# One reciprocal of eight columns for both units of a q tile, and the first token chunk's operands begun one queue turn later

## The chip, the cores and the metric

The kernel runs on one core of a Trainium2 chip. Its time is the device time of one execution in microseconds (us). The engines of the core work side by side, each through its own list of instructions in a fixed order: TensorE (PE in the profile, with the weight loads as PEld), VectorE (DVE), ScalarE (ACT), GpSimd (POOL) and SyncE (SP), which here only issues DMA transfers.

## The reference

A linear attention on random features feeds two feed-forward blocks without a residual. Scales of the inputs and shapes are left out where they don't matter.

```python
# attention: batch 4, heads 8, seq 576, head_dim 64, 128 features
phi(x) = exp(h - max(h)) / sqrt(128),  h = x @ omega.T - |x|^2 / 2      # x = q or k, scaled
q_p, k_p = phi(q), phi(k)
kv  = einsum('bhsm,bhsd->bhmd', k_p, v)
z   = sum(k_p, axis=2)
num = einsum('bhsm,bhmd->bhsd', q_p, kv)
den = einsum('bhsm,bhm->bhs', q_p, z)[..., None] + 1e-06
x   = (num / den) as [2304 tokens, 512]
# first block: 512 -> 2048 -> 512
x = softplus(x @ w_in) @ w_out
# second block: 512 -> 1024 (twice), 1024 -> 1024, 1024 -> 512
out = (((x @ w1) * (x @ w2)) @ w3) @ w_out
```

Everything is float32, and the output must be close to the float32 result.

## The kernel before, in words

**Precision and tiling.** A float32 product on TensorE is made of three matmuls of operands that were split into a high part (a rounded cast, name ending in h) and a low part (the value less its high part, name ending in l). Tokens are worked on in 18 q tiles of 128. The attention results of six tiles make one token chunk of 768, of which there are 3. The products of the feed-forward blocks go by Strassen-like quads: of each chunk of x four corner pieces (a11, a12, a21, a22) and four sums (s1 to s4) are made and split into high and low parts. All matmul results go to a pool of 8 PSUM banks (`ps()`, L83), so an early matmul often waits until VectorE or ScalarE has read a bank that is seven tiles old.

**Stages.** From 0 to 57 us the features of k and the sums kv are made, and weights are unpacked. From 57 to 150 us comes the q stage, on which the change acts. After it follow, on TensorE almost alone, the two feed-forward blocks, to 807 us.

**The q stage.** A tile has two units of 4 heads. For each unit, `q_feat` (L393) projects q (six matmuls), VectorE finds the row maximum (nmax, L349), and ScalarE applies four exponentials (qp, L354). `q_turn` (L406) transposes qp on TensorE (L409) and ScalarE copies the result (qpt, L411). `q_num` (L413) multiplies qpt with kv into one PSUM bank of 4 x 65 columns. The 65th column of each head is the denominator. VectorE adds a constant to the four denominators (den, L426), takes the reciprocal (L427, 128x4) and multiplies (xt, L430). `x_turn` (L435) transposes xt (L439), VectorE or ScalarE copies it (xs, L442 or L444), and SP stores it to xd in HBM (L445). The loop over tiles (L767) does step t of the projection, step t-2 of `q_turn`, t-3 of the numerators and t-4 of `x_turn`. In odd steps the numerators come first and in even steps last, so that the numerators of two tiles stand side by side on TensorE: 64 short matmuls into four banks.

**Operands of a chunk.** `operands` (L448) makes a list of small steps for a chunk: two loads of 768 KB from xd (xq, L455, into a pool of 2 buffers that all chunks share), then GAP empty steps (L483, only for chunks 0 and 1), then the casts on ScalarE (high parts, L469), the sums s1 to s4 on VectorE (L462) and the low parts on VectorE (L472). The first xq holds a11 and a21, the second a12 and a22. A queue takes some of these steps after each unit of the q stage (`step`, L241; JOB_Q = 0.5 steps a unit before the first chunk's list is there, 1.2 after). Chunk 0's list is queued after the turn of tile 5, chunk 1's after that of tile 11, chunk 2's behind the loop. In the loop's last steps (FILL, L754) the first quad (Up1 of chunk 0) is begun between the last tiles.

**Order.** The program is handed to a scheduler that sets the order on each engine from its own estimate, so a small change in the source can reorder instructions on several engines. Evictions of the quads (u, c and p: L517, L524, and the softplus L557) have a raised priority.

Of the kernel before, what the change touches and what calls it, by code (L numbers as in the profile page):

```python
# [19 lines left out]
F32 = mybir.dt.float32  # L20
# [4 lines left out]
ALU = mybir.AluOpType  # L25
AX = mybir.AxisListType

B, H, S, D = 4, 8, 576, 64
M = 128
NT = B * S  # L30
# [31 lines left out]
KEEP = 4  # L62
WARM = 3
WO_AHEAD = 3
GAP = 3
FILL = [18, 19, 20]
URGENT = 300
LINE = 32
# [3 lines left out]
def body(ctx: ExitStack, tc: tile.TileContext, q, k, k_rest, v, v_rest, om_t, w_in, w_out, w12, w3, wo, out):  # L72
    nc = tc.nc
    cp = ctx.enter_context(tc.tile_pool(name="cp", bufs=1))
    sm = ctx.enter_context(tc.tile_pool(name="sm", bufs=1))
    M_ = ctx.enter_context(tc.tile_pool(name="M_", bufs=14))
# [6 lines left out]
    def ps():  # L83
        return ps_.tile([128, 512], F32, tag="ps", name="ps")
# [7 lines left out]
    def tt(name):  # L92
        return T_.tile([128, 1024], F32, tag="t", name=name)

    def matmul(o, a, b, start, stop, **kw):
        nc.tensor.matmul(out=o, lhsT=a, rhs=b, start=start, stop=stop, **kw)  # L96
# [7 lines left out]
    xd = dr.tile([128, KD, NT], F32, name="xd")  # L104
# [10 lines left out]
    def take(pool, n):  # L115
        def ok():
            return free[pool] >= n

        return ok


    class Job:
# [5 lines left out]
        def load(self):  # L128
            self.raw = L_.tile([128, 4 * self.n], I16, tag="l", name="raw")
            (self.queue or nc.scalar).dma_start(out=self.raw[:, :4 * self.n - 1], in_=self.src.bitcast(I16)[:, 1:])  # L130
# [143 lines left out]
    def pair(name, bufs):  # L274
        n = small.get(name, (None, 1))[1]
        if n:
            small[name] = sm.tile([128, 2, 4], F32, tag=name, bufs=bufs, name=name), 0
        else:
            small[name] = small[name][0], 1
        return small[name][0][:, 1 - bool(n)]  # L280
# [6 lines left out]
    def xslot(pool, n, dt, name):  # L287
        return pools[pool].tile([128, n], dt, tag="x", name=name)

    kt, vt, kps, kpr, kvs, qts, kacc, raw = {}, {}, {}, {}, {}, {}, {}, {}  # L290
# [84 lines left out]
    def matmul_half(o, a, b, start, stop):  # L375
        for c in range(0, a.shape[-1], HALF):
            matmul(o[c:c + HALF], a[:, c:c + HALF], b, start, stop, skip_group_check=True)
# [11 lines left out]
        nc.scalar.copy(out=kvs[b][:, 4 * g:4 * g + 4, :], in_=acc)  # L389

    qp, qpt, xt = {}, {}, {}

    def q_feat(u):  # L393
        t, g = divmod(u, 2)
        p = project(lambda p: [x[:, 2 * g + p, :] for x in qts[t]])
        if g and t >= NT // 128 - len(EARLY):
            free["X0"] += 2

        def exps():
            qp[u] = M_.tile([128, 4, M], F32, tag="m", name="qp")  # L400
            features(*p, qp[u])

        waiting.append(exps)
        flush(QLAG)
# [5 lines left out]
        qpt[u] = M_.tile([128, 4, 128], F32, tag="m", name="qpt")  # L410
        nc.scalar.copy(out=qpt[u], in_=tp.rearrange("p (h t) -> p h t", h=4))  # L411

    def q_num(u):  # L413
        t, g = divmod(u, 2)
        nm = ps()
        nm = nm[:, 0:4 * (D + 1)].rearrange("p (h d) -> p h d", h=4)
        lo, hi = 128 * t, 128 * t + 128
        for h in range(4):
            a = lo
            while a < hi:  # L420
                b = a // S
                e = min(hi, (b + 1) * S)
                matmul_half(nm[a - lo:e - lo, h, :], qpt[u][:, h, a - lo:e - lo], kvs[b][:, 4 * g + h, :], True, True)
                a = e
        den = pair("den", 3)[:, :, None]
        nc.vector.tensor_scalar(out=den, in0=nm[:, :, D:D + 1], scalar1=1e-6 * M, scalar2=None, op0=ALU.add)  # L426
        nc.vector.reciprocal(out=den, in_=den)  # L427
        if g == 0:
            xt[t] = M_.tile([128, H, D], F32, tag="m", name="xt")
        nc.vector.tensor_tensor(  # L430
            out=xt[t][:, 4 * g:4 * g + 4, :], in0=nm[:, :, 0:D],
            in1=den.to_broadcast([128, 4, D]), op=ALU.mult,
        )

    def x_turn(t):  # L435
        tp = ps()
# [11 lines left out]
    def operands(c, src, pool):  # L448

        o, a, s = {}, [], {}  # L450

        def load(kk):
            def op():
                r = L_.tile([128, 2, 2 * N], F32, tag="l", name="xq")
                nc.sync.dma_start(out=r, in_=src[:, 2 * kk:2 * kk + 2, 2 * N * c:2 * N * (c + 1)])  # L455
                a.append([r[:, :, 0:N], r[:, :, N:2 * N]])
            return (op, lambda: stored[0] >= 2 * N * (c + 1)) if src is yd else op

        def total(name, x, y, op_):
            def op():  # L460
                s[name] = tt(name)[:, 0:2 * N].rearrange("p (k t) -> p k t", k=2)
                nc.vector.tensor_tensor(out=s[name], in0=x(), in1=y(), op=op_)  # L462
            return op

        def parts(name, x):
            def op_hi():
                free[pool] -= 2
                o[name] = [xslot(pool, 2 * N, FR, f"x{name}{w}").rearrange("p (k t) -> p k t", k=2) for w in "hl"]
                nc.scalar.copy(out=o[name][0], in_=x())  # L469

            def op_lo():
                nc.vector.tensor_tensor(out=o[name][1], in0=x(), in1=o[name][0].bitcast(F32), op=ALU.subtract)  # L472

            return [(op_hi, take(pool, 2)), op_lo]

        a11, a21 = lambda: a[0][0], lambda: a[0][1]
        a12, a22 = lambda: a[1][0], lambda: a[1][1]
        hi, lo = {}, {}
        for name, x in (("a11", a11), ("a12", a12), ("a22", a22), *((n, lambda n=n: s[n]) for n in ("s1", "s2", "s3", "s4"))):
            hi[name], lo[name] = parts(name, x)  # L480
        s1, s2 = total("s1", a21, a22, ALU.add), total("s2", lambda: s["s1"], a11, ALU.subtract)
        s3, s4 = total("s3", a11, a21, ALU.subtract), total("s4", a12, lambda: s["s2"], ALU.subtract)
        ops = [load(0), load(1)] + [lambda: None] * (GAP if src is xd and c < 2 else 0)  # L483
        if src is xd:
            ops += [hi["a11"], s3, lo["a11"], hi["s3"], s1, lo["s3"], s2, hi["s1"], hi["s2"], lo["s1"], lo["s2"]]
        else:
            ops += [hi["a11"], s1, lo["a11"], s2, s3, hi["s2"], lo["s2"], hi["s3"], hi["s1"], lo["s3"], lo["s1"]]
        ops += [hi["a12"], s4, lo["a12"], hi["a22"], hi["s4"], lo["a22"], lo["s4"]]
        ops.append(lambda: ready.add(c))
        return o, ops  # L490
# [260 lines left out]
    nt = NT // 128  # L751
    begun = None

    def fill():  # L754
# [3 lines left out]
            x = Up1(0, 0, UP_RATES["Up1"][0])  # L758
            begun = x, x.begin_parts()
        next(begun[1], None)  # L760

    def numerators(t):
        if 0 <= t < nt:
            for g in range(2):
                q_num(2 * t + g)

    for t in range(nt + XLAG):  # L767
        if t % 2:
            numerators(t - NLAG)
        for g in range(2):  # L770
            if 0 <= t - TLAG < nt:
                q_turn(2 * (t - TLAG) + g)
        for g in range(2):
            if t < nt:
                q_feat(2 * t + g)
            else:
                flush(0)
            step(JOB_Q[0 in xo])
        for x in [nt - len(EARLY) + n for n, at in enumerate(EARLY) if at == t] + [t + 2] * (t + 2 < nt - len(EARLY)):
            split_q(x)  # L780
            load_q()
        if t == 1:
            kv_sum(2 * B - 1)
            kstack.close()
            pools["X0"] = ctx.enter_context(tc.tile_pool(name="X0", bufs=28, side="right", reuse_waits="tile"))
        if t >= XLAG:
            x_turn(t - XLAG)
            for c in range(2):
                if t - XLAG == 2 * N // 128 * (c + 1) - 1:
                    xo[c], ops = operands(c, xd, "X0")  # L790
                    queue += ops
        if not t % 2:
            numerators(t - NLAG)
        if t in FILL:
            fill()
# [3 lines left out]

    pools["X1"] = ctx.enter_context(tc.tile_pool(name="X1", bufs=14, side="right", reuse_waits="tile"))  # L800
    xo[2], ops = operands(2, xd, "X1")
    queue += ops + job_ops(win[2:])

# [52 lines left out]
    for c in range(2):  # L856
        xo[c], ops = operands(c, yd, f"X{1 - c}")
        queue += ops
# [363 lines left out]
```

## Time and profile before

| What | Value |
|---|---|
| Median of 3 runs (lowest, highest) | 811.22 us (810.95, 811.86) |
| The profiled execution's own time | 813.02 us |
| Its span in the profile | 810.9 us |
| TensorE busy | 804.0 us, 99% of the span |
| VectorE, ScalarE, GpSimd busy | 602.3 us (74%), 441.2 us (54%), 26.5 us (3%) |
| Instructions on VectorE | 1022 |
| Granted TensorE clock | full speed (1.00) in every stretch shown |

The profiled execution takes 1.8 us more than the median, and 2.1 us of it lie outside the span. An engine's share is an average over stages. Where TensorE is busy all the time, another engine's speed decides nothing; in the q stage, VectorE and ScalarE are nearly as full as TensorE, and there short waits appear.

### The profile page before, as it was taken

What the parts mean: (1) busy time and instruction counts of PE and PEld (TensorE: products, weight loads), DVE (VectorE), ACT (ScalarE), POOL (GpSimd) and SP (SyncE); (2) the same over time, 40 slices, a digit from 0 to 9 for tenths busy, and PEclk for the clock granted to TensorE, in tenths of its full rate; (3) what the DMA queues carried; (4) which work ended last, traced back from release to release, by engine and by line L of the source; (5) the groups of instructions that cost most, each with busy time, mean ns of one, the idle gap of its engine ahead of it and who ended that gap; (6) DMA issues with size and microseconds to landing.
All of it is one profiled execution on the core that took longest, in us unless ns stands there. A gap on an engine that the chain in (4) does not pass through costs nothing.

```text
span 810.9 us, 14465 instructions
## 1 busy us (share of the span) xinstructions
PE 804.0 (99%) x5462; PEld 752.4 (93%) x5462; DVE 602.3 (74%) x1022; ACT 441.2 (54%) x859; POOL 26.5 (3%) x29
## 2 busy tenths in 40 slices
PE   9999999999999999999999999999999999999998
PEld 8999999999999998888888889999999998889998
DVE  6999999878765676754569633897988876888861
ACT  6999998557445676646456432424335123674330
POOL 3033300000000000000000000000000000000000
PEclk9999999999999999999999999999999999999999
DMA  9833635656535558688994642365656556353212
GB/s 288 327 100 87 201 107 172 210 205 214 195 133 195 191 193 259 214 258 293 335 304 148 208 127 79 133 217 186 209 174 214 188 180 237 111 170 122 73 65 78
DMA packets 75861, 150.04 MB, mean 185 GB/s; under 512 B 7184, under 2 KB 44688, under 8 KB 75792
## 3 DMA queue, kind: packets, MB, share of 16 engines
q1 hardware_dynamic: 64016, 101.55, 38.1%
q10 hardware_dynamic: 11776, 47.57, 17.4%
q8 instruction: 43, 0.70, 0.4%
q14 instruction: 26, 0.21, 0.1%
HBM read 98.24 MB, written 50.86 MB: 184 GB/s over the span
## 4 chain that ended last, share of the span: by engine, by line
PE 92%; DVE 4%; DMA 2%; issue 1%; ACT 0%; POOL 0%; ACTq 0%; POOLq 0%
PE ps L96 90%; DMA xq<-xd 1%; PE ps L409 1%; DVE nmax L349 1%; DVE xt L430 1%; DVE s L462 1%; PE ps L439 0%; DVE c L517 0%; DMA rawq<-in_q 0%; DVE u L517 0%; DVE xa22l L472 0%; DVE xa12l L472 0%; DVE qt L297 0%; DVE qtl L298 0%; DVE tlo L191 0%
## 5 line engine op out<-in xcount | busy, mean ns | idle before, releaser
L96 PE MATMUL ps<-dhi,lo 128*128 128x512 f32 x256 | 99.6, 389 | 0.0
L96 PE MATMUL ps<-dlo,hi 128*128 128x512 f32 x256 | 99.6, 389 | 0.0
L96 PE MATMUL ps<-dhi,hi 128*128 128x512 f32 x256 | 99.4, 389 | 0.0
L642 DVE TENSOR_TENSOR dlo<-dn,dhi 128x512 fp32r<-128x512 f32 x64 | 43.8, 689 | 39.1 <-ACT dhi L641 23.0
L517 DVE TENSOR_TENSOR c<-ps,u 128x384 f32<-128x384 f32 x144 | 71.5, 550 | 0.8
L517 DVE TENSOR_TENSOR u<-ps,p 128x384 f32<-128x384 f32 x48 | 26.7, 556 | 53.9 <-PE ps L96 52.3
L524 ACT COPY p<-ps 128x384 f32<-128x384 f32 x48 | 23.0, 480 | 75.8 <-PE ps L96 57.3
L641 ACT CAST dhi<-dn 128x512 fp32r<-128x512 f32 x64 | 39.4, 619 | 45.2 <-DVE dlo L642 25.7
L142 DVE SCALAR_TENSOR_TENSOR f<-raw,f 128x1024 int32<-128x1024 f32 (+2 forms) x43 | 45.5, 1058 | 20.3 <-ACT raw L139 18.8
L557 ACT ACTIVATE c<-c 128x384 f32<-128x384 f32 x72 | 35.1, 524 | 46.8 <-DVE c L517 43.0
L96 PEld LDWEIGHTS ps<-dlo,hi 128*128 128x128 f32 x256 | 48.1, 188 | 10.0
L96 PEld LDWEIGHTS ps<-dhi,hi 128*128 128x128 f32 x256 | 48.1, 188 | 10.0
L96 PEld LDWEIGHTS ps<-dhi,lo 128*128 128x128 f32 x256 | 48.1, 188 | 9.8
L138 ACT ACTIVATE f<-raw,bias 128x1024 f32<-128x1024 int16 (+2 forms) x43 | 46.3, 1084 | 18.9 <-DMA raw<-in_w 9.3
L349 DVE TENSOR_REDUCE nmax<-ps 128x4 f32<-128x512 f32 x72 | 47.0, 683 | 6.2 <-PE ps L96 6.0
L139 ACT ACTIVATE raw<-raw,bias 128x1024 f32<-128x1024 int16 (+2 forms) x43 | 46.3, 1082 | 0.6
L148 DVE SCALAR_TENSOR_TENSOR f<-raw,f 128x1024 int32<-128x1024 int32 (+2 forms) x43 | 45.0, 1046 | 0.6
L354 ACT ACTIVATE qp<-ps,nmax 128x128 f32<-128x128 f32 x144 | 42.2, 457 | 2.4 <-DVE nmax L349 2.4
L354 ACT ACTIVATE kp<-ps,nmax 128x128 f32<-128x128 f32 x128 | 35.5, 460 | 6.0 <-DVE nmax L349 5.9
L96 PE MATMUL ps<-xs1h,thi 128*128 128x384 f32 x96 | 32.4, 337 | 0.2 <-DVE c L517 0.2
L96 PE MATMUL ps<-xs2h,thi 128*128 128x384 f32 x96 | 32.3, 336 | 0.0
L96 PE MATMUL ps<-xs2h,tlo 128*128 128x384 f32 x96 | 32.2, 335 | 0.0
(257 smaller groups left out, 2339.4 us busy)
## 6 DMA issues: line engine op xcount, KB each, us to landing
dn<-gd SPq DMA_DIRECT2D x64, 256.0 KB, 4.0
raw<-in_w ACTq DMA_DIRECT2D x16, 1023.8 KB, 5.8
gd<-c SPq DMA_DIRECT2D x80, 192.0 KB, 2.7
pd<-c SPq DMA_DIRECT2D x48, 192.0 KB, 2.7
raw<-in_w_out ACTq DMA_DIRECT2D x10, 767.8 KB, 4.6
raw<-in_w_in ACTq DMA_DIRECT2D x6, 1023.8 KB, 5.1
rawq<-in_q SPq DMA_DIRECT2D x18, 256.0 KB, 3.1
xd<-xs SPq DMA_DIRECT2D x18, 256.0 KB, 3.3
```

Of the source, the lines that this page charges most:

```text
L96: nc.tensor.matmul(out=o, lhsT=a, rhs=b, start=start, stop=stop, **kw)
L138: nc.scalar.activation(out=self.f, in_=top, func=AF.Relu, scale=TOP, bias=bias[:, 0:1])
L139: nc.scalar.activation(out=self.words(1, F32, 2), in_=top, func=AF.Identity, scale=TOP, bias=bias[:, 1:2])
L142: nc.vector.scalar_tensor_tensor(out=self.f.bitcast(I32), in0=self.words(1, F32, 2), scalar=-2.0 ** 31, in1=self.f, op0=ALU.max, op1=ALU.min)
L148: nc.vector.scalar_tensor_tensor(out=fi, in0=self.words(0, I32, 2), scalar=13, in1=fi, op0=ALU.logical_shift_right, op1=ALU.bitwise_or,)
L349: nc.vector.tensor_reduce(out=nmax, in_=pj, axis=AX.X, op=ALU.max, negate=True)
L354: nc.scalar.activation(out=dst[:, h, :], in_=pj[:, h, :], func=AF.Exp, bias=nmax[:, h:h + 1])
L517: nc.vector.tensor_tensor(out=z, in0=bank, in1=y, op=ALU.add)
L524: nc.scalar.copy(out=p6, in_=b1)
L557: nc.scalar.activation(out=dst, in_=src, func=AF.Softplus)
L641: nc.scalar.copy(out=hi, in_=got[m])
L642: nc.vector.tensor_tensor(out=lo, in0=got.pop(m), in1=hi.bitcast(F32), op=ALU.subtract)
```

## The change

**Numerators.** The function `numerators` takes over from `q_num`. It issues the matmuls of both units of a tile, into two banks, then two denominator additions into one tile of 128x8, one reciprocal of 128x8, and the two multiplications. So 36 reciprocals of 128x4 become 18 of 128x8, and both banks are in use until the reciprocal is done.

**The gap.** GAP goes from 3 to 4 and the list of a chunk gets GAP - c empty steps: 4 in place of 3 for chunk 0, 3 as before for chunk 1. With 2.4 steps a tile, the first chunk's casts and sums are issued a little under half a tile later in program order.

```diff
--- before.py
+++ after.py
@@ -62,7 +62,7 @@
 KEEP = 4
 WARM = 3
 WO_AHEAD = 3
-GAP = 3
+GAP = 4
 FILL = [18, 19, 20]
 URGENT = 300
 LINE = 32
@@ -389,6 +389,7 @@
         nc.scalar.copy(out=kvs[b][:, 4 * g:4 * g + 4, :], in_=acc)
 
     qp, qpt, xt = {}, {}, {}
+    nt = NT // 128
 
     def q_feat(u):
         t, g = divmod(u, 2)
@@ -410,27 +411,31 @@
         qpt[u] = M_.tile([128, 4, 128], F32, tag="m", name="qpt")
         nc.scalar.copy(out=qpt[u], in_=tp.rearrange("p (h t) -> p h t", h=4))
 
-    def q_num(u):
-        t, g = divmod(u, 2)
-        nm = ps()
-        nm = nm[:, 0:4 * (D + 1)].rearrange("p (h d) -> p h d", h=4)
+    def numerators(t):
+        if not 0 <= t < nt:
+            return
+        nms = []
         lo, hi = 128 * t, 128 * t + 128
-        for h in range(4):
-            a = lo
-            while a < hi:
-                b = a // S
-                e = min(hi, (b + 1) * S)
-                matmul_half(nm[a - lo:e - lo, h, :], qpt[u][:, h, a - lo:e - lo], kvs[b][:, 4 * g + h, :], True, True)
-                a = e
-        den = pair("den", 3)[:, :, None]
-        nc.vector.tensor_scalar(out=den, in0=nm[:, :, D:D + 1], scalar1=1e-6 * M, scalar2=None, op0=ALU.add)
+        for g in range(2):
+            nm = ps()[:, 0:4 * (D + 1)].rearrange("p (h d) -> p h d", h=4)
+            for h in range(4):
+                a = lo
+                while a < hi:
+                    b = a // S
+                    e = min(hi, (b + 1) * S)
+                    matmul_half(nm[a - lo:e - lo, h, :], qpt[2 * t + g][:, h, a - lo:e - lo], kvs[b][:, 4 * g + h, :], True, True)
+                    a = e
+            nms.append(nm)
+        den = sm.tile([128, 2, 4, 1], F32, tag="den", bufs=3, name="den")
+        for g in range(2):
+            nc.vector.tensor_scalar(out=den[:, g], in0=nms[g][:, :, D:D + 1], scalar1=1e-6 * M, scalar2=None, op0=ALU.add)
         nc.vector.reciprocal(out=den, in_=den)
-        if g == 0:
-            xt[t] = M_.tile([128, H, D], F32, tag="m", name="xt")
-        nc.vector.tensor_tensor(
-            out=xt[t][:, 4 * g:4 * g + 4, :], in0=nm[:, :, 0:D],
-            in1=den.to_broadcast([128, 4, D]), op=ALU.mult,
-        )
+        xt[t] = M_.tile([128, H, D], F32, tag="m", name="xt")
+        for g in range(2):
+            nc.vector.tensor_tensor(
+                out=xt[t][:, 4 * g:4 * g + 4, :], in0=nms[g][:, :, 0:D],
+                in1=den[:, g].to_broadcast([128, 4, D]), op=ALU.mult,
+            )
 
     def x_turn(t):
         tp = ps()
@@ -480,7 +485,7 @@
             hi[name], lo[name] = parts(name, x)
         s1, s2 = total("s1", a21, a22, ALU.add), total("s2", lambda: s["s1"], a11, ALU.subtract)
         s3, s4 = total("s3", a11, a21, ALU.subtract), total("s4", a12, lambda: s["s2"], ALU.subtract)
-        ops = [load(0), load(1)] + [lambda: None] * (GAP if src is xd and c < 2 else 0)
+        ops = [load(0), load(1)] + [lambda: None] * (GAP - c if src is xd and c < 2 else 0)
         if src is xd:
             ops += [hi["a11"], s3, lo["a11"], hi["s3"], s1, lo["s3"], s2, hi["s1"], hi["s2"], lo["s1"], lo["s2"]]
         else:
@@ -759,11 +764,6 @@
             begun = x, x.begin_parts()
         next(begun[1], None)
 
-    def numerators(t):
-        if 0 <= t < nt:
-            for g in range(2):
-                q_num(2 * t + g)
-
     for t in range(nt + XLAG):
         if t % 2:
             numerators(t - NLAG)
```

**What moves on the engines.** TensorE's order is nearly the same. Three places on the other engines follow; numbers behind a name tell instances apart.

The first is VectorE near 75.5 to 79.5 us of the profile before, at the numerators of two neighbouring tiles: each xt frees one of their four banks; qt, qth and qtl are splits of the q tiles, nmax is a row maximum, and lo a part of a weight that is unpacked. Before:

```order
L297 CAST qt2_1016<-rawq_1262 128x512
L426 TENSOR_SCALAR den_1443<-ps_1434 128x4
L297 CAST qt0_898<-rawq_1369 128x512
L427 RECIPROCAL den_1443<-den_1443 128x4
L426 TENSOR_SCALAR den_1443<-ps_1448 128x4
L430 TENSOR_TENSOR xt_1446<-ps_1434,den_1443 128x256
L427 RECIPROCAL den_1443<-den_1443 128x4
L426 TENSOR_SCALAR den_1469<-ps_1460 128x4
L430 TENSOR_TENSOR xt_1446<-ps_1448,den_1443 128x256
L427 RECIPROCAL den_1469<-den_1469 128x4
L426 TENSOR_SCALAR den_1469<-ps_1474 128x4
L430 TENSOR_TENSOR xt_1472<-ps_1460,den_1469 128x256
```

The same place after the change:

```order
L431 TENSOR_SCALAR den_1449<-ps_1431 128x4
L297 CAST qt0_898<-rawq_1366 128x512
L298 TENSOR_TENSOR qtl_1684<-rawq_1526,qth_1683 128x512
L431 TENSOR_SCALAR den_1449<-ps_1440 128x4
L431 TENSOR_SCALAR den_1474<-ps_1456 128x4
L432 RECIPROCAL den_1449<-den_1449 128x8
L297 CAST qth_1746<-rawq_1687 128x512
L435 TENSOR_TENSOR xt_1453<-ps_1431,den_1449 128x256
L435 TENSOR_TENSOR xt_1453<-ps_1440,den_1449 128x256
L431 TENSOR_SCALAR den_1474<-ps_1465 128x4
L298 TENSOR_TENSOR qtl_1747<-rawq_1687,qth_1746 128x512
L432 RECIPROCAL den_1474<-den_1474 128x8
```

Behind the first denominator there now stand two low parts of q tiles (qtl) and one more cast (qth); lo moved ahead of the place shown, and the second tile's two multiplications follow the last row, with a row maximum ahead of them (before, three of the four multiplications were done by the last row). At the next pair of tiles, near 85 us, the qtl that stood between the first denominator and its reciprocal is gone.

The second is ScalarE near 96 to 104 us, where the operands of chunk 0 begin: xa11h, xs3h and xs1h are their high parts, xs the copies of turned tiles. Before:

```order
L354 ACTIVATE qp_1865<-ps_1843,nmax_1850 128x128 x4
L469 CAST xa11h_1870<-xq_1736 128x768
L411 COPY qpt_1888<-ps_1883 128x512
L411 COPY qpt_1895<-ps_1890 128x512
L354 ACTIVATE qp_1906<-ps_1857,nmax_1850 128x128 x4
L354 ACTIVATE qp_1921<-ps_1897,nmax_1904 128x128 x4
L469 CAST xs3h_1927<-s3_1911 128x768
L444 COPY xs_1937<-ps_1932 128x512
L411 COPY qpt_1997<-ps_1992 128x512
L411 COPY qpt_2004<-ps_1999 128x512
```

After:

```order
L354 ACTIVATE qp_1856<-ps_1834,nmax_1841 128x128 x4
L412 COPY qpt_1876<-ps_1871 128x512
L412 COPY qpt_1883<-ps_1878 128x512
L354 ACTIVATE qp_1894<-ps_1848,nmax_1841 128x128 x4
L474 CAST xa11h_1899<-xq_1729 128x768
L354 ACTIVATE qp_1910<-ps_1885,nmax_1892 128x128 x4
L449 COPY xs_1925<-ps_1920 128x512
L474 CAST xs3h_2006<-s3_1915 128x768
L474 CAST xs1h_2162<-s1_2022 128x768
L412 COPY qpt_1983<-ps_1978 128x512
L412 COPY qpt_1990<-ps_1985 128x512
```

The cast xa11h moved behind two copies and one set of exponentials, the copy xs moved ahead of xs3h, and xs1h came from further down.

The third is VectorE near 122 to 130 us, in the last tiles, where the buffers of chunk 0 come free for chunk 1. xa22l of 23xx is the last reader of chunk 0's second load, and s1 of chunk 1 is the first reader of chunk 1's second load. Before:

```order
L462 TENSOR_TENSOR s3_2492<-xq_2429 128x768
L472 TENSOR_TENSOR xa22l_2353<-xq_1738,xa22h_2352 128x768
L472 TENSOR_TENSOR xs4l_2356<-s4_2248,xs4h_2355 128x768
L442 COPY xs_2392<-ps_2387 128x512
L426 TENSOR_SCALAR den_2404<-ps_2395 128x4
L426 TENSOR_SCALAR den_2404<-ps_2409 128x4
L427 RECIPROCAL den_2404<-den_2404 128x4
L426 TENSOR_SCALAR den_2443<-ps_2434 128x4
L430 TENSOR_TENSOR xt_2407<-ps_2395,den_2404 128x256
L427 RECIPROCAL den_2404<-den_2404 128x4
L427 RECIPROCAL den_2443<-den_2443 128x4
L426 TENSOR_SCALAR den_2443<-ps_2448 128x4
```

After:

```order
L431 TENSOR_SCALAR den_2436<-ps_2418 128x4
L431 TENSOR_SCALAR den_2436<-ps_2427 128x4
L477 TENSOR_TENSOR xa22l_2338<-xq_1731,xa22h_2337 128x768
L477 TENSOR_TENSOR xs4l_2368<-s4_2321,xs4h_2367 128x768
L432 RECIPROCAL den_2436<-den_2436 128x8
L477 TENSOR_TENSOR xa11l_2473<-xq_2413,xa11h_2472 128x768
L435 TENSOR_TENSOR xt_2440<-ps_2418,den_2436 128x256
L435 TENSOR_TENSOR xt_2440<-ps_2427,den_2436 128x256
L477 TENSOR_TENSOR xs3l_2479<-s3_2475,xs3h_2478 128x768
L431 TENSOR_SCALAR den_2507<-ps_2489 128x4
L431 TENSOR_SCALAR den_2507<-ps_2498 128x4
L467 TENSOR_TENSOR s1_2521<-xq_2413,xq_2415 128x768
```

xa22l moved from ahead of the copy xs to a place behind the denominators of two tiles (xt_2401 and xt_2440 after the change are xt_2407 and xt_2446 before). s1, which before stands six rows behind those shown and ahead of the last tile's denominators, now stands behind the last tile's denominators, and behind it stand the last tile's reciprocal, s2 and then its two multiplications; before, s2 stood behind the first of the two.

On SP, the store of one more tile stands ahead of chunk 1's first load, and both loads of chunk 2 now stand ahead of the first stores of the quads' results (gd).

## Rows read from the trace of the kernel before

**Rows 1.** The page: busy time of each engine (share of the span) x instructions.
```profile
PE 804.0 (99%) x5462; PEld 752.4 (93%) x5462; DVE 602.3 (74%) x1022; ACT 441.2 (54%) x859; POOL 26.5 (3%) x29
```
**Rows 2.** Waits of TensorE, whole span: line waited for, total us, times, longest.
```profile
PE ps L409 <- ACT qp L354: 0.6, 2, 0.4
PE ps L96 <- ACT xs L444: 0.6, 1, 0.6
PE ps L96 <- DVE den L426: 0.4, 1, 0.4
PE ps L439 <- DVE den L427: 0.3, 1, 0.3
PE ps L96 <- DVE c L517: 0.2, 1, 0.2
```
**Rows 3.** Window: length; busy PE, PEld, DVE, ACT, POOL; clock, DMA share, GB/s.
```profile
76.00:86.00 10.00, 9.63 (x146) 8.82 (x140) 9.95 (x28) 9.36 (x31) 4.97 (x4) 1.00 0.46 127
```
**Rows 4.** VectorE's lines, 57 to 150 us: busy us, mean ns | idle before.
```profile
L427 DVE RECIPROCAL den<-den 128x4 f32<-128x4 f32 x36 | 5.8, 168 | 0.1
```
**Rows 5.** Timeline of VectorE, 117 to 118 us: start, duration (us), instruction.
```profile
117.31 0.22 DVE L426 TENSOR_SCALAR den<-ps 128x4 f32<-128x4 f32 x2
117.50 0.18 DVE L427 RECIPROCAL den<-den 128x4 f32<-128x4 f32 x1
...
117.71 0.42 DVE L430 TENSOR_TENSOR xt<-ps,den 128x256 f32<-128x256 f32 x1
```
**Rows 6.** Timeline of VectorE, 75 to 86 us.
```profile
75.98 0.15 DVE L426 TENSOR_SCALAR den<-ps 128x4 f32<-128x4 f32 x1
...
77.67 0.42 DVE L430 TENSOR_TENSOR xt<-ps,den 128x256 f32<-128x256 f32 x1
...
82.11 1.50 DVE L297 CAST qth<-rawq 128x512 fp32r<-128x512 f32 x1
83.54 1.27 DVE L349 TENSOR_REDUCE nmax<-ps 128x4 f32<-128x512 f32 x2
84.73 0.41 DVE L297 CAST qt<-rawq 128x512 fp32r<-128x512 f32 x1
85.07 0.15 DVE L426 TENSOR_SCALAR den<-ps 128x4 f32<-128x4 f32 x1
85.14 0.68 DVE L298 TENSOR_TENSOR qtl<-rawq,qth 128x512 fp32r<-128x512 f32 x1
85.74 0.17 DVE L427 RECIPROCAL den<-den 128x4 f32<-128x4 f32 x1
```
**Rows 7.** Timeline of TensorE at 79.6 us.
```profile
79.63 1.04 PE L409 MATMUL ps<-ident,qp 128*128 128x128 f32 x8
```
**Rows 8.** Timeline of ScalarE, 97.9 to 103.1 us; brackets: idle before, releaser.
```profile
97.97 0.84 ACT L469 CAST xa11h<-xq 128x768 fp32r<-128x768 f32 x1 [0.75 <-DMA xq<-xd]
...
101.68 0.90 ACT L469 CAST xs3h<-s 128x768 fp32r<-128x768 f32 x1
102.40 0.66 ACT L444 COPY xs<-ps 128x512 f32<-128x512 f32 x1
```
**Rows 9.** Timeline of TensorE at 124.2 us.
```profile
124.17 1.15 PE L96 MATMUL ps<-kv,qpt 128*64 128x65 f32 x32
```
**Rows 10.** The chain that ended last, 122 to 148 us: start, us, what.
```profile
122.84 0.88 DVE xa22l L472
...
123.74 4.94 DMA xq<-xd
...
128.70 0.96 DVE s L462
...
130.73 0.41 DVE xt L430
131.14 0.09 DVE den L427
...
140.84 7.08 DMA xq<-xd
```

## The prediction

> **What bounds the kernel now.** I read the page first: TensorE is busy for 804.0 us of the span, 99% [rows 1]. So a change can win only TensorE's short waits, and it loses whatever it adds to them. The list of TensorE's waits names all that can be won [rows 2]: 0.6 us in two waits on exponentials (qp), 0.6 us on a copy of a turned tile (xs), 0.4 us put down to a denominator, 0.3 and 0.2 us at the end of the q stage. That is 2.1 us. The timelines of TensorE place them. The 0.4 and the longer qp wait (0.4) lie together near 85.5 us (site A), the xs wait and the shorter qp wait (0.2) near 102 us (site B), the 0.3 at 131.3 us (site C) and the 0.2 at 149.9 us (site D). Then I read the windows: around A, VectorE has 9.95 of 10 us of work beside TensorE's 9.63 [rows 3], so there a microsecond of VectorE matters. Last I read the chain, which at the end of the q stage runs through loads of 768 KB: xq landed 4.94 and 7.08 us after its issue [rows 10].
>
> **The reciprocals.** 36 reciprocals of 128x4 take 168 ns each, 5.8 us in all [rows 4]; 18 of 128x8 stay. A reciprocal does not hold its successor for that long: the chain gives it 0.09 us [rows 10]. Removing 18 saves 18 x 0.09 = 1.6 us of VectorE. Against it, the multiplication that needs a reciprocal starts 0.21 us behind it (117.50 to 117.71 [rows 5]); before, the next denominator ran in that hole, and after the change the multiplication often stands right behind its reciprocal. If that holds for all 18 tiles, it costs 18 x (0.21 - 0.09) = 2.2 us, a balance of +0.6. The trace has no reciprocal of 128x8; twice the width in an instruction that short I bound by 0 and by another 0.17. So VectorE's own balance is between -1.6 and +0.6 us, or up to 3.1 us (18 x 0.17) more with the slow bound. I take 0, because holes of 0.1 us are filled in some tiles and not in others. Outside sites A to D none of it reaches TensorE, which covers it with its own matmuls.
>
> The Trainium skill, in "VectorE: DVE Perf Modes", sections "The DRAIN you can't avoid" and "Rules for kernel authors", says that the next operation waits until the pipe is empty, so that the count of operations is what to lower. By that, 18 fewer would give 18 x 0.168 = 3.0 us of VectorE, and sites A and B would clear as in the first rival; the row of 0.09 us speaks for half as much, and I give the rule no more weight than that rival's chance.
>
> **Site A, two neighbouring tiles' numerators.** The low part qtl between the first denominator and its reciprocal is gone there: it took from 85.14 to 85.74, 0.60 us [rows 6]. Both waits at A (0.8 us) should go. But the qtl and a cast were moved to the pair of tiles before, between 76 and 80 us. I count there, from the first denominator at 75.98 [rows 6], the order after the change with slots from starts of the same rows: a denominator 0.07, a cast 0.34 (84.73 to 85.07), a qtl 0.60, a row maximum 0.60 (two in 83.54 to 84.73), a reciprocal 0.09, a multiplication 0.34 like the cast, since both last 0.42. Up to the third multiplication come four denominators (0.28), two casts (0.68), two qtl (1.20), two reciprocals (0.18), two multiplications (0.68) and one row maximum (0.60): 3.62 us. It starts at 79.60 and ends at 80.02, where before it started at 77.67 [rows 6]. TensorE's transposes of qp need the bank that it frees and start at 79.63 without a wait [rows 7]. So about 0.5 us appear there (0.4, and 0.1 for the signal). Site A together: -0.8 + 0.5 = -0.3 us. Below, -0.8 if the pair before runs earlier than I count. Above: one cast in this stretch took 1.50 us in place of 0.42 [rows 6], with a split on GpSimd beside it, and the order now puts other casts there. One more such collision gives 0.5 + 1.1 - 0.8 = +0.8.
>
> **Site B, chunk 0's first operands.** Half a tile later, xa11h no longer waits 0.75 us on ScalarE for its load, and the copy xs stands ahead of xs3h, which took 0.72 us before it (101.68 to 102.40 [rows 8]). TensorE waited 0.6 us for xs and 0.2 for qp. Both are smaller than what ScalarE gains ahead of them, so B gives -0.8; 0 at the other end, if something else is late next there, most likely the sum s3, on which VectorE waits for the same load.
>
> **Site C, the last tiles.** Here the later operands cost. The second load of chunk 1 needs the buffer that xa22l of chunk 0 frees. Before, xa22l began at 122.84 and the load went out at 123.74 [rows 10]. After, xa22l stands behind the denominators of two tiles, and the last of these needs the 32 kv matmuls that TensorE ran from 124.17 for 1.15 us [rows 9]. So xa22l can begin at 125.45, end 0.88 later at 126.33, and the load goes out 2.6 us later than before. With 4.94 us it lands at 131.3. Before, the load released s1 at 128.70. After the change s1 stands at the head of VectorE's list with the last tile's reciprocal, s2 and both multiplications queued behind it: 131.3 + 0.88 + 0.09 + 0.88 (sums of the same shape as xa22l) gives the first multiplication at 133.15, against 130.73 [rows 10]. TensorE's transposes of the last tile wait for it, and TensorE had 0.3 us of waiting there already [rows 2], so +2.4 us goes straight onto its path. The lower end: even with the load in place, VectorE has xs4l, a reciprocal, xa11l, two multiplications, xs3l and two denominators ahead of s1, 3.55 us from 126.33, so s1 at 129.9, 1.2 later than 128.70, of which s2's new place and xs3l's give back 0.2: +1.0. The upper end: 7.08 us, as chunk 2's second load took: +4.5. Nothing below +1.0 unless xa22l itself comes earlier, which I price in the first rival. I take 2.4, the same transfer's own row.
>
> **Site D and the rest.** Both loads of chunk 2 now go out ahead of the quads' first stores, but s1 of chunk 2 still stands ahead of an eviction (c) on VectorE. TensorE waited 0.2 us there [rows 2]: I take 0, with -0.2 and +0.4 as ends (twice the row). The extra empty turn itself is not an instruction; the stores ahead of chunk 1's first load delay only that load, which the casts behind it don't need for some tiles.
>
> **The sum.** -0.3 (A) - 0.8 (B) + 2.4 (C) + 0 (D and reciprocals) = +1.3 us. The profiled execution took 813.02 us, so it would take 814.3; it stood 1.8 us above the median of the runs, 811.22, and the same 1.3 us on that gives 812.5.
>
> **Rivals.** *First, the operands come late without harm.* C assumes that xa22l waits for the denominators. If TensorE's lead there lets VectorE reach it sooner, or the load lands in about 2.5 us less, C costs nothing and its 0.3 goes too. With A (-0.8) and B (-0.8) and D (-0.2) gone: -2.1, 809.1 us. For it: all these waits are short and each has one VectorE or ScalarE instruction to blame that moves off. Against: the denominators' place in the list is fixed, and no xq of the chain landed in less than 4.9 us.
>
> *Second, slower: s1 at the head of VectorE's list waits for a slow load.* The load of chunk 1 goes out nearer to the stores of the last tiles; with the 7.08 us that chunk 2's took, C costs 4.5 in place of 2.4, and the sum is 813.02 + 3.4, by the median 814.6. It decides from a landing of about 5.3 us on, where the sum passes the 1.6 us that can be told. For it: the two rows of the same size differ by 2.1 us. Against: the nearer row, the same load, is the shorter one.
>
> *Third, the change doesn't do what it says.* The reciprocals removed lie beside TensorE's work, new short waits replace old ones at A and B, and the scheduler's moves cancel: 811.2 us. For it: each term but C is under 1 us, and C rests on one wait.
>
> **How the numbers follow.** A difference of 0.2%, 1.6 us, is about what a measurement of this kernel can tell from none. The forecast has 0.47: its +1.3 lies just inside that, so 0.26 of it counts as the same, 0.19 as slower and 0.02 as faster. The first rival has 0.24 (0.22 faster, 0.02 same), the second 0.14 (slower), the third 0.15 (same). Faster 0.24, same 0.43, slower 0.33. The range goes from 808.9, which takes in most of the first rival, to 814.8, just over the second; the likeliest case alone has 811.2 to 814.
>
> **What would show it.** In the profile after, the waits near 85.5 and 102 us are gone or smaller; a new one of about 0.5 us on a multiplication stands near 80 us; the second load of chunk 1 goes out some 2.6 us later against TensorE's kv matmuls; s1 of chunk 1 waits for it on VectorE by 1 us or more; and TensorE's transposes of the last xt wait for some 2.5 us. I am wrong if that last wait stays under 1 us, or if TensorE waits longer between 60 and 100 us than before.

## The result and the profile after

| | Before | After |
|---|---|---|
| Median of 5 runs (lowest, highest) | 811.52 us (810.95, 812.37) | 815.67 us (815.15, 816.9) |
| Ratio to before, 95% interval | 1 | 1.0054 (1.004 to 1.0068) |
| Profiled execution, span | 813.02, 810.9 us | 815.67, 813.5 us |
| Instructions on VectorE | 1022 | 1004 |

The change makes the kernel slower by 4.4 us by the ratio (0.0054 x 812). The forecast was 812.5 us, with a range up to 814.8: the side was right as far as the forecast took one (+1.3 us), the size was not, and the measured time lies outside the range. The spans of the two profiled executions differ by only 2.6 us, because the one of before stood 1.5 us above its median and the one of after stands on it.

The page after, engines' busy time as in [rows 1], and below it the waits of TensorE as in [rows 2]:

```profile
PE 803.4 (99%) x5462; PEld 752.5 (92%) x5462; DVE 600.1 (74%) x1004; ACT 442.0 (54%) x859; POOL 26.5 (3%) x29
```
```profile
PE ps L444 <- DVE xt L435: 2.1, 2, 1.2
PE ps L410 <- DVE xt L435: 1.2, 4, 0.6
PE ps L410 <- ACT qp L354: 1.0, 2, 0.7
...
PE ps L96 <- DVE xt L435: 0.7, 1, 0.7
PE ps L96 <- issue: 0.3, 1, 0.3
PE ps L96 <- ACT kp L354: 0.2, 1, 0.2
```

VectorE has 2.2 us less work, as the change meant, and TensorE about as much as before (803.4 against 804.0 us). The waits, 2.1 us before, are 5.5 us now, and 4.0 us of them are waits for xt, the multiplications behind the reciprocal. Both sums leave out a wait of 0.9 us on GpSimd at the start of the program, which is the same in both profiles; neither the rows above nor [rows 2] show it. The largest of these waits on TensorE's timeline:

```profile
65.62 0.33 PE L410 MATMUL ps<-ident,qp 128*128 128x128 f32 x1 [0.68 <-ACT qp L354]
...
80.30 0.36 PE L96 MATMUL ps<-omh,qt 128*128 128x256 f32 x1 [0.73 <-DVE xt L435]
...
82.30 0.73 PE L410 MATMUL ps<-ident,qp 128*128 128x128 f32 x5 [0.60 <-DVE xt L435]
...
88.04 0.63 PE L410 MATMUL ps<-ident,qp 128*128 128x128 f32 x4 [0.19 <-DVE xt L435]
...
130.34 0.41 PE L444 MATMUL ps<-ident,xt 128*128 128x128 f32 x2 [0.89 <-DVE xt L435]
...
134.91 0.44 PE L444 MATMUL ps<-ident,xt 128*128 128x128 f32 x2 [1.21 <-DVE xt L435]
```

The waits at 80 and 82 us belong to the pair of tiles of [rows 6, 7], those at 130 and 135 us to the last two tiles of [rows 9, 10]. VectorE's timeline at the first place, where the xt of 77.67 in [rows 6] stood before:

```profile
77.69 0.20 DVE L432 RECIPROCAL den<-den 128x8 f32<-128x8 f32 x1
79.40 0.43 DVE L297 CAST qth<-rawq 128x512 fp32r<-128x512 f32 x1 [1.51 <-DMA rawq<-in_q]
79.74 0.75 DVE L435 TENSOR_TENSOR xt<-ps,den 128x256 f32<-128x256 f32 x2
80.40 0.15 DVE L431 TENSOR_SCALAR den<-ps 128x4 f32<-128x4 f32 x1
80.47 0.68 DVE L298 TENSOR_TENSOR qtl<-rawq,qth 128x512 fp32r<-128x512 f32 x1
81.07 0.20 DVE L432 RECIPROCAL den<-den 128x8 f32<-128x8 f32 x1
81.18 0.64 DVE L349 TENSOR_REDUCE nmax<-ps 128x4 f32<-128x512 f32 x1
81.74 0.74 DVE L435 TENSOR_TENSOR xt<-ps,den 128x256 f32<-128x256 f32 x2
```

The reciprocal is done at 77.89, but its multiplications start at 79.74: between them stands a cast that waits 1.51 us for a load of q. The next reciprocal has a row maximum between itself and its multiplications. The same engine at the second place, where [rows 10] showed s1 at 128.70 and xt at 130.73:

```profile
126.99 0.16 DVE L431 TENSOR_SCALAR den<-ps 128x4 f32<-128x4 f32 x1 [0.30 <-PE ps L96]
127.07 0.95 DVE L477 TENSOR_TENSOR xa22l<-xq,xa22h 128x768 fp32r<-128x768 f32 x1
127.97 0.96 DVE L477 TENSOR_TENSOR xs4l<-s,xs4h 128x768 fp32r<-128x768 f32 x1
128.84 0.20 DVE L432 RECIPROCAL den<-den 128x8 f32<-128x8 f32 x1
128.96 0.91 DVE L477 TENSOR_TENSOR xa11l<-xq,xa11h 128x768 fp32r<-128x768 f32 x1
129.78 0.75 DVE L435 TENSOR_TENSOR xt<-ps,den 128x256 f32<-128x256 f32 x2
...
132.50 0.16 DVE L431 TENSOR_SCALAR den<-ps 128x4 f32<-128x4 f32 x1 [0.30 <-PE ps L96]
132.57 0.95 DVE L467 TENSOR_TENSOR s<-xq 128x768 f32<-128x768 f32 x1
133.44 0.20 DVE L432 RECIPROCAL den<-den 128x8 f32<-128x8 f32 x1
133.56 0.96 DVE L467 TENSOR_TENSOR s<-s,xq 128x768 f32<-128x768 f32 x1
134.44 0.75 DVE L435 TENSOR_TENSOR xt<-ps,den 128x256 f32<-128x256 f32 x2
```

s1 at 132.57 follows the denominator at once: there is no wait for the second load of chunk 1, on which the forecast built. Again one long instruction stands between each reciprocal and its xt (xa11l, then s2), and others ahead of the reciprocal (xa22l and xs4l, then s1).

Over the whole q stage of this profile, 7 of the 18 reciprocals have such a stranger behind them (an instruction that has nothing to do with the numerators, 0.37 to 0.96 us long), 3 have a denominator of the next tile, and 8 have nothing. Six of TensorE's seven waits on xt, all but 0.2 of the 4.0 us, come at a tile with a stranger. Strangers are not new, though: before, 11 of the 36 reciprocals had one, and no wait of TensorE was put down to an xt. The last tile before, behind its first unit's xt at 130.73 [rows 10]:

```profile
131.06 0.17 DVE L427 RECIPROCAL den<-den 128x4 f32<-128x4 f32 x1
131.15 0.93 DVE L462 TENSOR_TENSOR s<-s,xq 128x768 f32<-128x768 f32 x1
131.99 0.42 DVE L430 TENSOR_TENSOR xt<-ps,den 128x256 f32<-128x256 f32 x1
```

The same s2 stood in a hole there, but only one unit's multiplication waited behind it. Now both units' do.

### The profile page after: what moved, and what is told of

It reads as the page before. It is cut to its first block, busy times and chain, and to the rows that moved or that the text cites. A ratio compares the mean times of both kernels' runs of the same rounds, so it can differ in the third digit from the quotient of the medians.

```text
span 813.5 us, 14450 instructions
## 1 busy us (share of the span) xinstructions
PE 803.4 (99%) x5462; PEld 752.5 (92%) x5462; DVE 600.1 (74%) x1004; ACT 442.0 (54%) x859; POOL 26.5 (3%) x29
## 4 chain that ended last, share of the span: by engine, by line
PE 89%; DVE 4%; ACT 4%; DMA 2%; issue 1%; SPq 0%; POOL 0%; DVEq 0%; ACTq 0%; POOLq 0%
PE ps L96 87%; ACT kp L354 2%; DVE nmax L349 1%; ACT qp L354 1%; DMA xq<-xd 1%; PE ps L410 1%; DVE xt L435 1%; DVE s L467 1%; PE ps L444 0%; DMA rawq<-in_q 0%; ACT qpt L412 0%; DMA xd<-xs 0%; ACT f L138 0%; ACT raw L139 0%; ACT thi L187 0%
## 5 line engine op out<-in xcount | busy, mean ns | idle before, releaser
L187 ACT CAST thi<-t 128x1024 fp32r<-128x1024 f32 x16 | 17.2, 1077 | 28.6 <-PE ps L96 25.5
```

## The theories

**Hole.** A multiplication cannot start until the reciprocal's result is there, some 0.2 us (117.50 to 117.71 in [rows 5]). With a reciprocal per unit the other unit's denominator or reciprocal stands in most of these holes. With one for both units nothing of this tile's numerators is left, and the scheduler puts in whatever it takes to be ready: a cast, a row maximum, an operand of 0.4 to 0.9 us, one of which waits for a load. Both of the tile's multiplications then wait. **Gap.** The loss comes from the operands that begin a turn later. **Banks.** It comes from asking for both units' banks before either is read.

## The experiments

Each was timed in 5 rounds or more beside the kernel before; the ratio is to that one. The kernel before had a median of 812.33 us beside the first four experiments and 812.43 beside the last four, 0.8 to 0.9 us more than in the table above, from which the expectations in us were made. So an expectation in us is better read as a ratio to 811.52: read so, one reciprocal with the old gap, the gap alone and two reciprocals in the last tiles come inside the ranges of the hole theory, though in us they lie 0.6 to 0.9 above them.

**One reciprocal with the old gap.** GAP = 3 for both chunks, as before; the numerators as in the change.

```diff
-GAP = 4
+GAP = 3
-        ops = [load(0), load(1)] + [lambda: None] * (GAP - c if src is xd and c < 2 else 0)
+        ops = [load(0), load(1)] + [lambda: None] * (GAP if src is xd and c < 2 else 0)
```


> The kernel after the change with the gap of before (three empty turns for chunks 0 and 1), so only the numerators are changed. Three theories. Hole: one reciprocal per tile leaves 0.2 us between itself and its multiplications in which nothing of the numerators can run, the scheduler puts whatever is ready there (casts, maxima, sums of 0.4 to 0.9 us), and the banks come free late; then nearly the whole loss comes with this part: 815 to 816.5 us, the load wait of about 1.5 us near 79 us and waits of the last two tiles' transposes on xt of 1 to 2 us in all stay. Gap: the loss comes from the operands that begin later; then 811 to 812 us and no long wait on the last tiles' xt. Banks: both banks are held until the second denominator is done; then the loss is spread over all pairs of tiles and this run is as slow as the changed kernel.

817.44 us, 1.0061 (1.0049 to 1.0073). The waits at 80 and 82 us are 0.73 and 0.60 us, VectorE's load wait 1.50 us. All of the loss is there without the gap; the gap theory's 811 to 812 us fell. By the time alone the run does not tell the hole from the banks, for which the same was expected; but TensorE's waits on xt stand at four places and not at all pairs of tiles. In the last tile TensorE waited 1.59 us for xt; at the second to last the wait was put down to a copy of ScalarE (0.78 us).

**The gap alone.** The kernel before with the changed gap.

```diff
-GAP = 3
+GAP = 4
-        ops = [load(0), load(1)] + [lambda: None] * (GAP if src is xd and c < 2 else 0)
+        ops = [load(0), load(1)] + [lambda: None] * (GAP - c if src is xd and c < 2 else 0)
```


> The kernel before with only the gap changed (four empty turns for chunk 0, three for chunk 1). Hole and banks: no loss here, 810 to 811.7 us; the waits near 102 us (0.8 us) are gone, and the last tiles' transposes wait for xt at most 0.5 us. Gap: 814.5 to 816 us with the waits of the last tiles' transposes on xt of the changed kernel, 2 us.

812.27 us, 1.0001 (0.9992 to 1.0011): no difference. Near 102 us the wait for xs is gone, as forecast; TensorE waits there only 0.19 us:

```profile
103.32 0.36 PE L96 MATMUL ps<-omh,qt 128*128 128x256 f32 x1 [0.19 <-DVE den L426]
...
130.88 0.41 PE L439 MATMUL ps<-ident,xt 128*128 128x128 f32 x2 [0.36 <-DVE den L427]
```

The second row answers to the 0.3 us of before in [rows 2]: the gap does no harm in the last tiles. What it saves near 102 us is too little for the runs to show.

**Two reciprocals per tile.** The changed kernel, with the reciprocal split and nothing else.

```diff
-        nc.vector.reciprocal(out=den, in_=den)
+        for g in range(2):
+            nc.vector.reciprocal(out=den[:, g], in_=den[:, g])
```


> The changed kernel with two reciprocals of 128x4 per tile in place of one of 128x8; both units' matmuls, the common denominator tile and the gap stay. Hole: the first multiplication no longer waits for the second denominator and the second reciprocal fills the hole of the first, so the order goes back to about that of the kernel before and the time to 810 to 812 us; s1 and s2 of chunk 1 stand behind the last tile's multiplications. Banks and gap: both banks are still asked for together and the gap is still four, so the time stays at 814.5 to 816.5 us.

813.82 us, 1.0017 (1.0008 to 1.0027). This is three parts in five or more of the loss undone by adding 18 instructions; it did not come down quite to the level of before. The last tiles' waits are 0.23 us. At the pair near 86 us there is still something in a hole, and the rows show it:

```profile
86.66 0.18 DVE L433 RECIPROCAL den<-den 128x4 f32<-128x4 f32 x1
86.75 1.23 DVE L297 CAST qth<-rawq 128x512 fp32r<-128x512 f32 x1
87.90 0.17 DVE L433 RECIPROCAL den<-den 128x4 f32<-128x4 f32 x1
87.99 0.72 DVE L436 TENSOR_TENSOR xt<-ps,den 128x256 f32<-128x256 f32 x2
```

A cast of 1.23 us stands between the tile's two reciprocals, and both multiplications wait behind the second. TensorE waited 0.75 us for xt there. So a stranger also gets in between two reciprocals of a tile. Neither theory's range was met: 0.0017 x 812 = 1.4 us of the loss is left (0.6 to 2.2 by the interval), and this run alone does not separate the common order of the denominators from the banks.

**Two reciprocals in the last two tiles only.**

```diff
-        nc.vector.reciprocal(out=den, in_=den)
+        if t < nt - 2:
+            nc.vector.reciprocal(out=den, in_=den)
+        else:
+            for g in range(2):
+                nc.vector.reciprocal(out=den[:, g], in_=den[:, g])
```


> The changed kernel with two reciprocals only in the last two tiles. Hole: the two waits of the last tiles' transposes on xt (0.89 and 1.21 us in the profile after) shrink to under 0.5 us together, everything up to 120 us stays, so 1.5 to 2.1 us less than the changed kernel: 813.6 to 814.2 us. Gap and banks: these waits stay, 815.2 to 816.2 us.

814.78 us, 1.0031 (1.0019 to 1.0043). VectorE at the last tile:

```profile
132.85 0.15 DVE L431 TENSOR_SCALAR den<-ps 128x4 f32<-128x4 f32 x1
132.93 0.30 DVE L436 RECIPROCAL den<-den 128x4 f32<-128x4 f32 x2
133.14 0.74 DVE L439 TENSOR_TENSOR xt<-ps,den 128x256 f32<-128x256 f32 x2
133.80 0.95 DVE L471 TENSOR_TENSOR s<-xq 128x768 f32<-128x768 f32 x1
134.78 0.96 DVE L471 TENSOR_TENSOR s<-s,xq 128x768 f32<-128x768 f32 x1
```

The second reciprocal fills the hole, the multiplications follow, and s1 and s2 stand behind them. TensorE's waits on the last two tiles' xt fell from 2.1 to 0.2 us. Against the changed kernel's 1.0054 (1.0044 when it ran again beside the last four) that is 1.1 to 1.9 us, and 1.9 us in waits. The intervals of the times overlap, so here it is the waits that tell; in time the same edit shows in the run of both edits below.

**The late q tiles' splits one step later.** The cast with the load wait belongs to one of the last q tiles; this moves it off the pair near 78 us.

```diff
-EARLY = [9, 10, 10]
+EARLY = [9, 11, 11]
```


> The changed kernel with the splits of the last two q tiles one and two steps later in the program (EARLY 9, 11, 11 in place of 9, 10, 10), so that no cast that waits for a load of rawq stands between the reciprocal and the multiplications near 79 us. Hole theory: the load wait of VectorE of 1.5 us there goes, and with it TensorE's waits of 0.73 and 0.60 us; the casts come back near 88 us and cost up to 0.5 us there: 0.8 to 1.3 us less than the changed kernel, a ratio to the kernel before of 1.0038 to 1.0044. If that load wait was covered by something else, the two waits stay and the ratio is 1.005 or more.

814.28 us, 1.0025 (1.0016 to 1.0034): a larger gain than was expected, 2.4 us against the changed kernel's 1.0054 and 1.5 us against its 1.0044 in the same rounds. At the pair that had the load wait:

```profile
77.54 0.22 DVE L431 TENSOR_SCALAR den<-ps 128x4 f32<-128x4 f32 x2
77.73 0.20 DVE L432 RECIPROCAL den<-den 128x8 f32<-128x8 f32 x1
77.97 0.75 DVE L435 TENSOR_TENSOR xt<-ps,den 128x256 f32<-128x256 f32 x2
78.64 0.15 DVE L431 TENSOR_SCALAR den<-ps 128x4 f32<-128x4 f32 x1
78.83 0.20 DVE L432 RECIPROCAL den<-den 128x8 f32<-128x8 f32 x1
79.06 0.75 DVE L435 TENSOR_TENSOR xt<-ps,den 128x256 f32<-128x256 f32 x2
...
81.60 1.49 DVE L297 CAST qth<-rawq 128x512 fp32r<-128x512 f32 x1 [0.22 <-DMA rawq<-in_q]
```

Now nothing stands between the reciprocals and their multiplications (rows left out lie between the last two). The cast runs at 81.6 and waits for its load 0.22 us, where TensorE does not wait for it. TensorE's waits at 80, 82 and 88 us (1.5 us) are gone; those at 129 and 134 us stay, 0.89 and 1.18, and one of 0.35 us on xt near 103 us is new. The edit also moves a low part (qtl) and a row maximum from this pair, so its gain is not the load's alone.

**Both.** The last two edits together.

> The later splits and two reciprocals in the last two tiles, together, on the changed kernel. If the two causes are separate, their gains add: 0.8 to 1.3 us and 1.9 us off the changed kernel's 4.4 us, a ratio of 1.0015 to 1.002; TensorE's waits on xt come to under 1 us in all. If they only hand on one another's slack, the ratio stays at the better one's, 1.003.

812.48 us, 1.0000 (0.9991 to 1.0009). All of the loss is gone, with one reciprocal in 16 of the 18 tiles and the gap still changed. TensorE's waits:

```profile
PE ps L410 <- ACT qp L354: 1.0, 2, 0.7
...
PE ps L410 <- DVE xt L439: 0.4, 2, 0.2
PE ps L96 <- DVE xt L439: 0.3, 1, 0.3
PE ps L448 <- DVE xt L439: 0.2, 1, 0.2
```

0.9 us of waits on xt are left of 4.0. The two gains add: 1.0054 less 0.0023 and 0.0029 would leave 1.0002, and by the changed kernel's 1.0044 it would be 1.0012, as far as the intervals can tell. That is better than the 1.0015 to 1.002 expected. The interval lies clear of that of each edit alone, so either edit gains when it is added to the other: 2.0 us for the last tiles (from 1.0025), 2.5 us for the later splits (from 1.0031).

The run also bears on the banks. It asks for both units' banks together in every tile, as the changed kernel does, and loses nothing, while strangers still stand in some holes (near 71, 104 and 112 us) where TensorE waits at most 0.22 us. So asking for both banks has no standing cost that the time shows. A stranger costs time only where TensorE needs the tile's banks or its xt at that moment.

**The later splits on the kernel before**, as a control (EARLY alone changed).

> The kernel before with the later splits alone. Its own waits at 85.5 us (0.8 us) had a low part of such a split between the first denominator and its reciprocal, and this moves it off: 0.4 to 0.8 us less than before, a ratio of 0.999 to 0.9995, if VectorE was late there for that reason; 1.000 if the wait on the exponentials at the same place sets it.

813.2 us, 1.0012 (1.0003 to 1.0021): slower, not faster. The waits at 85.5 us are gone, but others came near 100 and 117 us (0.27, 0.38 and 0.43 us). The profiled execution was the fastest of its eleven (811.57), so its trace does not show where the 0.0012 lie. So the edit is no gain of its own; on the changed kernel it undoes part of what the hole did.

**The changed kernel again.**

> The changed kernel once more, unchanged, beside the others: ratio 1.0045 to 1.006 to the kernel before, and in its profile the same waits on xt near 80, 82, 130 and 135 us (0.73, 0.60, 0.89 and 1.21 us) within 0.2 us, if they belong to the order and not to that one execution.

815.84 us, 1.0044 (1.0031 to 1.0058), just under the range. The four waits are 0.68, 0.60, 0.89 and 1.20 us: they belong to the order. The span of this profiled execution is 815.8 us, 2.3 longer than the first one's, and near 105 us there are waits that the first lacked:

```profile
104.60 0.66 PE L410 MATMUL ps<-ident,qp 128*128 128x128 f32 x4 [0.40 <-ACT qp L354]
...
105.75 0.39 PE L96 MATMUL ps<-omh,qt 128*128 128x256 f32 x1 [0.49 <-ACT xs L449]
```

That is site B, with the same two releasers as before the change. In this kernel the gap takes those waits away in one execution and not in another.

No version was found that beats both kernels.

## Why the prediction was wrong

**What bounds, and the waits as the currency: right.** TensorE's work did not change, and the loss is in its short waits.

**The reciprocals.** VectorE's balance of -1.6 to +0.6 us was sized from the right row, and the 128x8 costs little more than the 128x4:

```profile
L432 DVE RECIPROCAL den<-den 128x8 f32<-128x8 f32 x18 | 3.6, 200 | 0.2
```

200 ns against 168 in [rows 4]. The step that failed is the price of the hole behind it. The forecast took a hole as 0.21 us of emptiness, counted a filled one as costing nothing, and set the balance to 0 "because holes of 0.1 us are filled in some tiles and not in others". But what fills a hole holds both of the tile's multiplications, and so both banks, for its own length of 0.37 to 0.96 us and for any load that it waits for. That is where most of the loss comes from: TensorE's waits on xt went from none to 4.0 us, its other waits from 2.1 to 1.5, and the two edits that take strangers away at four tiles undo the whole loss in time. "Outside sites A to D none of it reaches TensorE" failed too, by 1.1 us: 0.68 at 65.6 us, 0.21 at 106 and 0.23 at 114. The forecast worked out from the Trainium skill's rule ("VectorE: DVE Perf Modes", "Rules for kernel authors") to lower the count of operations that VectorE would have 3.0 us less work; 2.2 us came, and the kernel was slower.

**Site A: -0.3 forecast, +0.7 in the profile.** The waits of before (0.8) went, and where 0.5 us was forecast, 0.73 + 0.60 + 0.19 = 1.5 us came on xt. My count of 3.62 us to the third multiplication was right as a count of work and left out that one of its two casts reads a load: VectorE waited 1.51 us there, and the multiplication came 5.27 us after the first denominator (76.47 to 81.74). The rows of the order that I showed had that cast, qth from rawq, directly between the reciprocal and xt. The trace before has a wait of the same kind, 0.96 us for a load of rawq between a reciprocal and its xt at 69 us, and the forecast had no term for it. The 0.68 us at 65.6 us lies outside the site and comes on the exponentials: a cast of a weight (thi), which ran at 68.8 us before, now stands ahead of them on ScalarE, at 63.0. That this cast is the reason is read from the order and not tested; the wait stays, 0.69 us, in the run with both edits.

**Site B: -0.8 forecast.** It came in the profile after (no wait near 102 us) and, but for 0.19 us, with the gap alone, yet not in the second profile of the changed kernel. So that the number was met is in part luck of the one execution. In the time, the gap is worth nothing that shows: 1.0001.

**Site C: +2.4 forecast, +1.8 in the profile (0.89 + 1.21 - 0.28), by half of the mechanism that I gave.** The second load of chunk 1 did go out late, 4.3 us later than in the profile before (128.04 against 123.74), or 2.7 us later against the 32 kv matmuls (125.79 against 124.17), where 2.6 was forecast. But s1 did not wait for it; it followed the last tile's denominator, for which VectorE had waited on TensorE. From s1 on the forecast held: s1, the reciprocal and s2 stood ahead of the multiplications and took 1.87 us (132.57 to 134.44), 1.85 forecast. The other half of the loss, 0.89 us at the tile before, had no term in the +2.4: xa22l, xs4l and xa11l stood in and ahead of the hole there. I had counted most of those for the lower end (+1.0). With two reciprocals in the last two tiles these instructions stand behind xt, and 1.9 of the 2.1 us are gone. The second rival, a slow load at s1, fell with that. That +1.8 lies near +2.4 is therefore partly luck. Site D went from 0.2 to 0.

**The signs.** Of the two signs of being wrong that the forecast named, the second came: TensorE's waits between 60 and 100 us went from 0.8 to 2.2 us. The last tile's wait, for which some 2.5 us was named, was 1.21, and s1's wait on the load was absent.

**The sum.** By the profile: A +0.7, B -0.8, C +1.8, D -0.2, and +1.1 at 65.6, 106 and 114 us, so +2.6, as the spans differ. (Waits of 0.8 us more, at 57.5 us and in the stage before, and 0.6 us less of TensorE's own busy time stand in no term and nearly cancel.) The other 1.5 us between this and the medians' 4.15 is the profiled execution of before, which stood that much above its median. I carried my sum over to the median as if both were shifted alike; the range should have been wider by that. Where those 1.5 us of that execution lie, the traces don't show.

**What stays open.** What the 1.4 us left with two reciprocals per tile are made of; a standing cost of the two banks asked for together is unlikely, since the run with both edits has it in every tile and its interval ends at 1.0009, 0.7 us. Why the scheduler takes a long instruction for the hole: its order shows that it does, no run shows the reason.

## What to carry to other kernels

When instructions are merged on an engine that a scheduler fills, ask what stood in the latency between the old ones: a dependent pair without an independent partner can get a stranger in between, and where another engine waits for the pair's result, the stranger's length, or the load that it waits for, is the price. Merging also puts more results behind the same stranger: here two units' instead of one's. Read the new order for each instruction between a producer and the consumer that another engine waits for, and for each of them what it waits for itself. And a sum worked out on one profiled execution needs that execution's distance from the median as a width of its range.

## What the runs showed of the hardware

A reciprocal of 128x8 took 200 ns, one of 128x4 168: twice the columns cost 32 ns. In the profile before, an instruction that did not need the reciprocal's result started 0.09 us after it (131.06 to 131.15 above), and one that did 0.21 us after it (117.50 to 117.71 [rows 5]); behind the 128x8 that was 0.24 us (77.73 to 77.97 with the later splits).

Casts and low parts of 128x512 on VectorE and splits of q tiles of the same size on GpSimd did not run side by side: between 57 and 105 us of all ten profiles, the one that began later took longer. The casts and low parts took 0.40 to 0.69 us alone or when they began first, and a split that began behind one then took up to 1.69 in place of 1.28 us. Where the split had begun first, a cast ended 0.3 us after it and a low part up to 0.6 us after it. So the cast at 81.60 above took 1.49 us beside a split from 81.52 to 82.82, and the longest low part 1.67. That is also how the cast between two reciprocals at 86.75 above became 1.23 us long.
